# A hand-ordered attention and max-out kernel: its list of units is replaced by another list

## The chip, the cores and the metric

The kernel runs on one core of a Trainium2 chip. The metric is the device time of one execution, in microseconds (us). Names of engines: PE is the matrix engine (PEld its weight loads), ACT the scalar engine, DVE the vector engine, POOL the general one, and SP the engine that here does nothing but give out transfers (DMAs).

## What is computed

Local attention with a few global keys, in 4 batches of 8 heads, 768 positions and 64 columns a head, and after it a layer that takes the maximum of three products and multiplies it by a fourth matrix:

```python
scores = scale * np.matmul(q, k.transpose(0, 1, 3, 2))
is_global = pos[None, :] < 8
is_local = (rel >= 0) & (rel < 96)
dist = np.where(is_global & ~is_local, 96.0, np.abs(rel))
scores = np.where(is_global | is_local, scores - slopes * dist, -1e9)
a = softmax(scores)                     # over the keys
x = np.matmul(a, v)                     # then [4 * 768, 8 * 64] = [3072, 512]
h = np.maximum(np.maximum(x @ w1, x @ w2), x @ w3)   # 512 -> 768
out = h @ w_out                         # 768 -> 512
```

## The kernel before

**Tiles.** The 3072 rows are 24 tiles of 128; tile T is batch T // 6, position T % 6 in it. A query tile needs only its own key tile and the one before it (96 local keys), and the 8 global keys, which are copied over the first 8 places of the previous key tile. For the second layer the tiles are gathered in 7 chunks, of 4, 2, 2, 4, 4, 4 and 4 tiles.

**Units.** The whole work is cut in small units. A string, `SCHEDULE` (L25), lists them by name, and the loop at L475 calls them one by one: this is the order of instructions on each engine, written out by hand, and each engine works through its own part of it in that order. So a unit that waits holds up all that stands behind it on the same engine, and on SP a transfer that waits holds up the later ones. Numbers behind a letter are the unit's arguments; the last one often names the engine of a copy (0 ACT, 1 DVE, 2 POOL).

| unit | line | what it does |
|---|---|---|
| l, L, v, w, o | 151, 160, 169, 412, 419 | SP: loads of q or k in parts (tiles 0 to 11), of q and k of one tile (tiles 12 to 23; two transfers), of v, of w1, w2, w3 (w0.j: 512 KB, w1.j: 1 MB), of w_out |
| c, C, W, Q | 178, 185, 425, 429 | casts to bf16 of these: c of a part, C T.0 of a tile's q and k (3: half on DVE, half on POOL), C T.1 of its v, W of w, Q of w_out |
| x | 226 | PE: 8 transposes of a part of q or k, then one copy to SBUF (0 and 2: ACT, 1 and 3: DVE) or two half copies, ACT and DVE (4 and up) |
| X | 245 | the same for a tile: 4 is a transpose by DMA, given out by SP; below 4 it is 8 transposes on PE and copies (1: DVE; 3: one half each on ACT and DVE) |
| S | 268 | PE: scores of four heads (g) of a tile; ACT: exp. With a last digit 1 the bias is added on PE first, with 0 the mask is left to M |
| M | 302 | DVE: exp of the scores times the mask |
| G, V | 209, 218 | copies of the 8 global keys or values into a tile's buffers, between the tile's own use and the next tile's |
| A | 311 | PE: attention times v; DVE: reciprocal and multiply (L331, L332), which give xb |
| T | 335 | transposes xb into the chunk's xT: 4 by DMA from SP, else 4 transposes on PE and a copy |
| F c.f.j | 355 | PE: product of chunk c with columns f of w1, w2 or w3 (j); j = 0: ACT copies it to h01; j = 1 and 2: DVE takes the maximum |
| O c.t | 385 | PE: a tile's product with w_out, six matmuls; copy by ACT or DVE; SP: store |
| E | 390 | the same for the last chunk, cut finer |
| B, K | 291, 297 | the bias and mask tables |
| D i.n | 432 | n matmuls of zeros, 128 columns each, whose result nobody reads |

**Buffers that tie units together.** F, O, D and some transposes share three PSUM buffers (psH, L116); one more is for transposes (psT, L117). Scores and A share two (sp0, sp1; the last digit of A says which). Six raw buffers take q and k (L103), six take v, five take the casts, three xb, six P (two a tile), four the stores.

Of the kernel before, what the change touches and what calls it, by code (L numbers as in the profile page):

```python
# [22 lines left out]


SCHEDULE = """  # L25
    B6.1 K5 B5.1 D0.54 l1.0 K6 c1.0.2 B4.1 B0.1 B2.1 K0 B3.0 B7.1 B1.1 c0.1.1 c0.0.0 x0.0.3 K4 x0.1.4 K7
    S0.1.1 S0.0.1 l1.1 c1.1.1 G0.0 S1.1.0 v0 C0.1.1 S1.0.1 G1.1 x1.0.3 M0.1 M0.0 x1.1.4 A0.1 M1.0 v1 v2
    S2.0.1 S2.1.0 G2.2 M1.1 S3.0.1 S3.1.1 C1.1.1 C2.1.2 M2.0 M2.1 l2.1 c2.1.1 A1.0 V1.2 K1 x2.1.4 v3
    T0.1 C3.1.2 A2.1 V2.0 l2.0 c2.0.0 G3.0 w0.0 T1.0 A3.0 x2.0.4 M3.0 w0.1 T2.0 T3.1 w0.2 W0.0.2 W0.2.1
    W0.1.2 S4.0.0 S4.1.0 M4.1 G4.0 F0.0.0 F0.1.0 F0.1.1 K2 F0.0.1 S5.0.0 S5.1.0 V3.2 w1.0 W1.0.1 F0.0.2  # L30
    K3 M5.0 F0.1.2 F0.3.0 M4.0 F0.2.0 w1.1 W1.1.1 W2.0.2 F0.5.0 F0.4.0 W2.1.2 F0.5.1 v4 C4.1.2 A4.0
    F0.4.1 M5.1 F0.3.1 w1.2 W2.2.0 W1.2.2 T4.1 V4.2 F0.2.1 M3.1 F0.5.2 v5 C5.1.0 A5.0 l3.1 c3.1.2 F0.3.2
    F0.2.2 T5.1 l3.0 c3.0.0 x3.1.3 F0.4.2 F1.0.0 F1.4.0 x3.0.4 F1.0.1 F1.0.2 l3.2 c3.2.2 x3.2.3 l3.3
    c3.3.2 F1.3.0 x3.3.1 G6.1 F1.2.0 F1.1.0 F1.1.1 S7.1.0 S7.0.0 G7.2 F1.2.1 F1.4.1 F1.1.2 F1.3.1 S6.1.0
    S6.0.0 F1.2.2 F1.5.0 o0 Q0.2 M6.1 o2 o1 v7 C7.1.2 M7.0 v6 C6.1.0 S8.1.0 S8.0.0 Q2.2 M6.0 v11 l4.1 v8
    v9 Q1.2 G8.1 l4.0 F1.3.2 M7.1 F1.5.1 F1.5.2 O0.2.0 M8.1 A6.1 T6.4 v10 A7.0 V7.2 T7.4 F1.4.2 L12 M8.0
    O0.0.0 S9.1.0 S9.0.0 c4.1.2 x4.1.4 O0.3.0 M9.1 c4.0.2 M9.0 L13 O0.1.0 L14 x4.0.4 C8.1.2 A8.1 F2.0.0
    F2.1.0 C11.1.0 F2.3.0 C10.1.1 T8.4 G9.2 S10.0.0 S10.1.0 C9.1.2 F2.1.1 V8.1 F2.0.1 F2.1.2 A9.0 V9.2
    G10.0 M10.0 F2.3.1 F2.3.2 S11.1.0 M11.1 M10.1 S11.0.0 M11.0 C12.0.2 O1.1.0 F2.2.0 F2.0.2 A10.0
    F2.2.1 V10.0 T9.4 F2.5.0 A11.1 F2.4.0 C13.0.2 X13.4 F2.2.2 T10.1 v13 X12.4 F2.5.1 G12.2 C14.0.2  # L40
    O1.0.0 T11.1 F2.4.1 F2.4.2 F3.0.0 F3.1.0 F3.0.1 F3.0.2 F3.1.1 F3.1.2 C13.1.1 v17 L15 C15.0.3
    S13.1.0 M13.1 v18 S13.0.0 M13.0 F3.3.0 G13.0 F3.2.0 F3.2.1 S12.0.0 S12.1.0 F3.2.2 F3.3.1 v12 C12.1.0
    A13.1 V13.2 v14 X14.4 L16 F2.5.2 F3.3.2 M12.1 C14.1.2 S14.0.0 M14.0 M12.0 S14.1.0 M14.1 F3.4.0
    F3.4.1 F3.5.0 L18 v15 A12.1 A14.0 X15.4 F3.4.2 L17 C17.1.2 C15.1.0 T12.4 C18.0.2 v16 C16.1.2 G14.1
    C18.1.2 T13.4 F3.5.1 T14.4 F3.5.2 C16.0.0 S15.1.0 M15.1 S15.0.0 X16.4 X18.4 G15.1 V14.1 L19 O3.2.1
    O3.1.0 M15.0 O3.3.0 C17.0.2 A15.1 V15.1 X17.4 O2.0.0 T15.1 S16.0.0 C19.0.2 S16.1.0 M16.1 O3.0.1
    M16.0 F4.0.0 F4.2.0 S18.1.0 L20 S18.0.0 C20.0.2 F4.0.1 F4.0.2 F4.4.0 A16.0 X19.4 L21 F4.5.0 M18.0
    F4.5.1 F4.5.2 G16.0 T16.4 S17.1.0 S17.0.0 F4.2.1 v19 v20 V16.0 X20.4 M18.1 C19.1.2 M17.1 M17.0
    F4.2.2 F4.1.0 F4.1.1 S19.1.0 S19.0.0 M19.1 L22 F4.3.0 C21.0.0 X21.4 M19.0 O2.1.1 F4.3.1 A18.1 T18.4
    A17.0 C22.0.0 T17.4 G18.1 F4.1.2 G19.2 F4.3.2 A19.1 T19.4 V19.2 v21 L23 F4.4.1 F4.4.2 S20.0.0 M20.0  # L50
    S20.1.0 G20.0 X22.4 O4.2.0 C23.0.2 X23.4 M20.1 C20.1.0 O4.0.0 S21.1.0 S21.0.0 M21.1 F5.0.0 F5.1.0
    A20.1 F5.2.0 F5.3.0 F5.2.1 G21.0 S22.1.0 M21.0 S22.0.0 G22.2 V20.2 M22.1 F5.1.1 F5.0.1 C21.1.1
    F5.0.2 M22.0 S23.1.0 S23.0.0 F5.4.0 F5.3.1 F5.4.1 F5.4.2 F5.2.2 T20.4 v23 v22 A21.0 C22.1.2 F5.1.2
    V21.2 M23.0 A22.1 T22.4 V22.1 M23.1 F5.3.2 C23.1.0 O4.1.0 F5.5.0 A23.1 T23.4 F5.5.1 T21.4 F5.5.2
    O5.0.0 O4.3.0 O5.2.0 F6.0.0 F6.4.0 F6.4.1 O5.3.1 F6.2.0 F6.2.1 O5.1.1 F6.2.2 F6.4.2 F6.0.1 F6.0.2
    F6.3.0 F6.3.1 F6.3.2 F6.5.0 F6.1.0 F6.1.1 F6.1.2 F6.5.1 F6.5.2 E D1.9
"""


# [450 lines left out]
```

## Time and profile before

| | |
|---|---|
| median of 3 runs | 188.74 us (188.74 to 188.77) |
| the profiled execution | 188.74 us, its span 187.0 us |
| DMA packets, bytes | 88931, 36.83 MB, mean 197 GB/s |
| SP's queue, share of 16 engines' time | 86.8% |
| F units on PE, 128x512 form | 347 matmuls recorded, 379 ns each |
| transposes by DMA | 12 of q and k (2.07 us of SP each, 4.5 us to land), 15 of xb (1.26 us, 2.8 us) |
| transposes on PE | 96 of q and k parts, 36 of xb |

The span runs from the first to the last instruction. "Busy" for PE is the time in which a matmul is in flight; matmuls overlap, so in a row the 379 ns of one take only some 0.216 us of PE's time (38 in 8.37 us). An arrow "A <- B: 4.9, 4, 1.9" says that A waited for B for 4.9 us in all, 4 times, 1.9 us at the longest. Columns of a stage line are told where it is shown.

### The profile page before, as it was taken

How to read it: one execution, taken by the hardware profiler on the slowest of the kernel's cores; microseconds unless marked ns; L12 is line 12 of the kernel's file. 1: busy time of each engine (PE TensorE's matmuls, PEld its weight loads, DVE VectorE, ACT ScalarE, POOL GpSimd, SP SyncE). 2: the span in 40 equal slices, each digit the busy share in tenths (PEclk: the TensorE clock that was granted, in tenths of full speed). 3: DMA queues.
4: the chain of work that ended last, by engine and by line, in shares of the span. 5: the costliest groups of instructions: out<-in, count | busy, mean ns of one | idle time of the engine just before them, and what ended most of it. 6: DMA issues, size and time to landing. Idle time of an engine off the chain costs nothing.

```text
span 187.0 us, 4000 instructions
## 1 busy us (share of the span) xinstructions
PE 169.2 (91%) x1550; PEld 99.1 (53%) x1571; DVE 126.0 (67%) x241; ACT 96.9 (52%) x155; POOL 37.9 (20%) x62
## 2 busy tenths in 40 slices
PE   7787899999999899999989699999859999999991
PEld 7653754558765678545545345454424554444450
DVE  5767868898799789478985257897457793256500
ACT  5677887623675675337645454644937322311240
POOL 4102426442527040021130420211021200000000
PEclk9997899999999999999999999999999999999999
DMA  5999999999885999999999999999797415220023
GB/s 142 290 236 233 303 383 342 320 360 308 211 199 137 186 294 174 230 222 167 226 208 140 181 287 261 148 220 242 157 167 171 85 44 152 112 112 4 0 100 126
DMA packets 88931, 36.83 MB, mean 197 GB/s; under 512 B 71504, under 2 KB 83664, under 8 KB 88912
## 3 DMA queue, kind: packets, MB, share of 16 engines
q1 hardware_dynamic: 88768, 36.51, 86.8%
q8 instruction: 12, 0.20, 0.4%
q14 instruction: 7, 0.06, 0.1%
q10 hardware_dynamic: 144, 0.07, 0.1%
HBM read 25.17 MB, written 6.29 MB: 168 GB/s over the span
## 4 chain that ended last, share of the span: by engine, by line
PE 46%; DMA 19%; DVE 18%; issue 7%; SPq 4%; ACT 3%; POOL 1%; ACTq 0%; DVEq 0%; POOLq 0%
PE h L361 30%; PE po L376 7%; DMA qkT<-qkb 6%; DVE qkT L243 4%; DMA xT<-xb 4%; PE sp L283 4%; DVE P L307 3%; DMA out_dram<-ost 3%; DVE xb L332 3%; DMA rawp<-in_k_dram 3%; SPq L167 3%; DVE ht L370 3%; DMA raw<-in_k_dram 3%; DVE h L368 2%; ACT P L288 2%
## 5 line engine op out<-in xcount | busy, mean ns | idle before, releaser
L361 PE MATMUL h<-xT,w 128*128 128x512 bf16 (+1 forms) x491 | 100.2, 348 | 2.4 <-DMA xT<-xb 1.4
L361 PEld LDWEIGHTS <-w 128*128 128x128 bf16 x504 | 46.8, 98 | 42.0 <-issue 2.3
L288 ACT ACTIVATE P<-sp 128x1024 bf16<-128x1024 f32 (+1 forms) x48 | 43.4, 953 | 19.2 <-PE sp L283 19.1
L368 DVE TENSOR_TENSOR h<-h,h 128x512 bf16<-128x512 bf16 (+1 forms) x42 | 25.4, 606 | 21.2 <-PE h L361 20.8
L307 DVE TENSOR_TENSOR P<-P,wmask 128x1024 bf16<-128x1024 bf16 x36 | 28.5, 799 | 11.8 <-ACT P L288 11.2
L366 ACT CAST h<-h 128x512 bf16<-128x512 f32 (+1 forms) x42 | 22.0, 530 | 26.6 <-PE h L361 25.9
L376 PE MATMUL po<-wo,ht 128*128 128x512 bf16 (+2 forms) x148 | 32.9, 362 | 0.8 <-DVE ht L370 0.2
L370 DVE TENSOR_TENSOR ht<-h,h 128x512 bf16<-128x512 bf16 (+1 forms) x42 | 25.3, 606 | 3.4 <-PE h L361 1.8
L382 ACT COPY ost<-po 128x512 f32<-128x512 f32 (+2 forms) x20 | 11.2, 563 | 24.2 <-PE po L376 22.5
L376 PEld LDWEIGHTS <-ht 128*128 128x128 bf16 x156 | 14.2, 98 | 15.5 <-DVE ht L370 1.0
L283 PE MATMUL sp<-qkT 64*128 64x128 bf16 x352 | 15.0, 219 | 7.7 <-DMA qkT<-qkb 4.9
L283 PEld LDWEIGHTS <-qkT 64*128 64x128 bf16 x352 | 10.3, 95 | 17.5 <-DMA qkT<-qkb 6.9
L332 DVE TENSOR_TENSOR xb<-op,rz 128x512 bf16<-128x512 f32 x24 | 16.6, 691 | 0.8
L322 PEld LDWEIGHTS <-P 128*128 128x128 bf16 x192 | 12.7, 99 | 3.0 <-issue 0.5
L322 PE MATMUL op<-va,P 128*128 128x65 bf16 x160 | 13.1, 196 | 0.3 <-DVE P L307 0.3
L198 POOL CAST qkb<-raw 128x1024 bf16<-128x1024 f32 x8 | 8.3, 1038 | 23.3 <-DMA raw<-in_k_dram 23.3
L189 POOL CAST va<-rawv 128x512 bf16<-128x512 f32 x11 | 7.3, 664 | 23.8 <-DMA rawv<-in_v_dram 19.4
L325 PEld LDWEIGHTS <-P 128*128 128x128 bf16 x160 | 10.9, 99 | 1.2
L243 DVE COPY qkT<-tpp 128x512 bf16<-128x512 bf16 (+1 forms) x12 | 10.6, 906 | 0.7 <-PE tpp L239 0.5
L325 PE MATMUL op<-va,P 128*128 128x65 bf16 x128 | 10.0, 193 | 0.3 <-ACT va L221 0.3
L382 DVE COPY ost<-po 128x512 f32<-128x512 f32 (+1 forms) x6 | 3.7, 621 | 7.3 <-PE po L376 5.7
L239 PE MATMUL tpp<-identb,qkp 128*128 128x128 bf16 x96 | 7.6, 227 | 0.6 <-ACT qkp L183 0.3
(64 smaller groups left out, 107.8 us busy)
## 6 DMA issues: line engine op xcount, KB each, us to landing
rawv<-in_v_dram SPq DMA_DIRECT2D x24, 256.0 KB, 5.6
out_dram<-ost SPq DMA_DIRECT2D x23, 256.0 KB, 3.0
rawp<-in_q_dram SPq DMA_DIRECT2D x6, 512.0 KB, 7.2
rawp<-in_k_dram SPq DMA_DIRECT2D x6, 512.0 KB, 7.1
wst<-in_moe_w_dram SPq DMA_DIRECT2D x3, 1024.0 KB, 12.1
raw<-in_q_dram SPq DMA_DIRECT2D x12, 256.0 KB, 4.5
raw<-in_k_dram SPq DMA_DIRECT2D x12, 256.0 KB, 5.0
wst<-in_moe_w_dram SPq DMA_DIRECT2D x3, 512.0 KB, 6.6
```

The costliest lines, as they stand in the source:

```text
L243: copy(dst[:, lo:hi], tp.rearrange("c e j i -> c j i e"))
L283: nc.tensor.matmul(sp[:, hh, j2, ds], qT(T - ds, 1)[hsl, jp], qT(T, 0)[hsl, jp], start=not how, stop=True, skip_group_check=True)
L288: nc.scalar.activation(P[:, :, 0:n], sp.rearrange("p a b d n -> p (a b) d n")[:, :, 0:n], AF.Exp, bias=0.0, scale=scale)
L307: nc.vector.tensor_mul(P, P, wmask[:, g, :, 0:2])
L322: nc.tensor.matmul(o, P[:, i, 0], heads(va[T])[:, h], start=True, stop=(t == 0), skip_group_check=True)
L325: nc.tensor.matmul(o, P[:, i, 1], heads(va[T - 1])[:, h], start=False, stop=True, skip_group_check=True)
L332: nc.vector.tensor_tensor(out=x.rearrange("p (g h) d -> p g h d", g=2), in0=o4[:, :, :, 0:64], in1=rz[:, :, :, None].to_broadcast([128, 2, ...
L361: nc.tensor.matmul(ps, w123[f // 2][:, dm, j, (f % 2) * 128:(f % 2) * 128 + 128], xT[c][:, dm], start=(dm == 0), stop=(dm == 3))
L366: nc.scalar.copy(h01, ps)
L368: nc.vector.tensor_max(h01s[c, f], h01s[c, f], ps)
L370: nc.vector.tensor_max(ht[c][:, f], h01s[c, f], ps)
L376: nc.tensor.matmul(po, ht[c][:, f, tt * 128:(tt + 1) * 128], wo[:, f, cols], start=(f == 0), stop=(f == NF - 1))
```

## The change

The string is replaced by another; no other line differs. The same units stand in it, but for the zero matmuls: D0.54 at the head and D1.9 at the end become D0.45 at the head and D1.4 between x0.0 and x0.1. The order is another throughout, and so are many engine digits:

| | before | after |
|---|---|---|
| X by DMA / on PE | 12 / 0 | 9 / 3 (X12.1, X16.3, X18.3) |
| T by DMA / on PE | 15 / 9 | 11 / 13 |
| x: ACT whole / DVE whole / halves | 0 / 5 / 7 | 6 / 3 / 3 |
| c by ACT / DVE / POOL | 3 / 3 / 6 | 1 / 4 / 7 |
| C of q and k, ACT / DVE / POOL / half and half | 3 / 0 / 8 / 1 | 2 / 3 / 7 / 0 |
| C of v, ACT / DVE / POOL | 7 / 5 / 12 | 10 / 4 / 10 |
| W, ACT / DVE / POOL | 1 / 3 / 5 | 4 / 2 / 3 |
| V that copy, ACT / DVE / POOL | 3 / 4 / 9 | 0 / 2 / 14 |
| A in sp0 / sp1 | 11 / 13 | 10 / 14 |

On SP the first loads stand as l1.0 l1.1 v0 v1 v2 l2.1 v3 l2.0 w0.0 w0.1 w0.2 w1.0 w1.1 before, and as l1.0 l1.1 v0 l2.0 l2.1 v1 v2 v3 w0.0 w1.0 w0.1 w0.2 v4 w1.1 after (l0.0 and l0.1 stand ahead of the list, in both). The diff, with parts of the old list left out and the new one whole:

```diff
-    B6.1 K5 B5.1 D0.54 l1.0 K6 c1.0.2 B4.1 B0.1 B2.1 K0 B3.0 B7.1 B1.1 c0.1.1 c0.0.0 x0.0.3 K4 x0.1.4 K7
-    S0.1.1 S0.0.1 l1.1 c1.1.1 G0.0 S1.1.0 v0 C0.1.1 S1.0.1 G1.1 x1.0.3 M0.1 M0.0 x1.1.4 A0.1 M1.0 v1 v2
-    S2.0.1 S2.1.0 G2.2 M1.1 S3.0.1 S3.1.1 C1.1.1 C2.1.2 M2.0 M2.1 l2.1 c2.1.1 A1.0 V1.2 K1 x2.1.4 v3
-    T0.1 C3.1.2 A2.1 V2.0 l2.0 c2.0.0 G3.0 w0.0 T1.0 A3.0 x2.0.4 M3.0 w0.1 T2.0 T3.1 w0.2 W0.0.2 W0.2.1
-    W0.1.2 S4.0.0 S4.1.0 M4.1 G4.0 F0.0.0 F0.1.0 F0.1.1 K2 F0.0.1 S5.0.0 S5.1.0 V3.2 w1.0 W1.0.1 F0.0.2
-    K3 M5.0 F0.1.2 F0.3.0 M4.0 F0.2.0 w1.1 W1.1.1 W2.0.2 F0.5.0 F0.4.0 W2.1.2 F0.5.1 v4 C4.1.2 A4.0
-    F0.4.1 M5.1 F0.3.1 w1.2 W2.2.0 W1.2.2 T4.1 V4.2 F0.2.1 M3.1 F0.5.2 v5 C5.1.0 A5.0 l3.1 c3.1.2 F0.3.2
-    F0.2.2 T5.1 l3.0 c3.0.0 x3.1.3 F0.4.2 F1.0.0 F1.4.0 x3.0.4 F1.0.1 F1.0.2 l3.2 c3.2.2 x3.2.3 l3.3
-    c3.3.2 F1.3.0 x3.3.1 G6.1 F1.2.0 F1.1.0 F1.1.1 S7.1.0 S7.0.0 G7.2 F1.2.1 F1.4.1 F1.1.2 F1.3.1 S6.1.0
...
-    A13.1 V13.2 v14 X14.4 L16 F2.5.2 F3.3.2 M12.1 C14.1.2 S14.0.0 M14.0 M12.0 S14.1.0 M14.1 F3.4.0
-    F3.4.1 F3.5.0 L18 v15 A12.1 A14.0 X15.4 F3.4.2 L17 C17.1.2 C15.1.0 T12.4 C18.0.2 v16 C16.1.2 G14.1
-    C18.1.2 T13.4 F3.5.1 T14.4 F3.5.2 C16.0.0 S15.1.0 M15.1 S15.0.0 X16.4 X18.4 G15.1 V14.1 L19 O3.2.1
...
-    C18.1.2 T13.4 F3.5.1 T14.4 F3.5.2 C16.0.0 S15.1.0 M15.1 S15.0.0 X16.4 X18.4 G15.1 V14.1 L19 O3.2.1
-    O3.1.0 M15.0 O3.3.0 C17.0.2 A15.1 V15.1 X17.4 O2.0.0 T15.1 S16.0.0 C19.0.2 S16.1.0 M16.1 O3.0.1
-    M16.0 F4.0.0 F4.2.0 S18.1.0 L20 S18.0.0 C20.0.2 F4.0.1 F4.0.2 F4.4.0 A16.0 X19.4 L21 F4.5.0 M18.0
-    F4.5.1 F4.5.2 G16.0 T16.4 S17.1.0 S17.0.0 F4.2.1 v19 v20 V16.0 X20.4 M18.1 C19.1.2 M17.1 M17.0
-    F4.2.2 F4.1.0 F4.1.1 S19.1.0 S19.0.0 M19.1 L22 F4.3.0 C21.0.0 X21.4 M19.0 O2.1.1 F4.3.1 A18.1 T18.4
-    A17.0 C22.0.0 T17.4 G18.1 F4.1.2 G19.2 F4.3.2 A19.1 T19.4 V19.2 v21 L23 F4.4.1 F4.4.2 S20.0.0 M20.0
-    S20.1.0 G20.0 X22.4 O4.2.0 C23.0.2 X23.4 M20.1 C20.1.0 O4.0.0 S21.1.0 S21.0.0 M21.1 F5.0.0 F5.1.0
-    A20.1 F5.2.0 F5.3.0 F5.2.1 G21.0 S22.1.0 M21.0 S22.0.0 G22.2 V20.2 M22.1 F5.1.1 F5.0.1 C21.1.1
-    F5.0.2 M22.0 S23.1.0 S23.0.0 F5.4.0 F5.3.1 F5.4.1 F5.4.2 F5.2.2 T20.4 v23 v22 A21.0 C22.1.2 F5.1.2
-    V21.2 M23.0 A22.1 T22.4 V22.1 M23.1 F5.3.2 C23.1.0 O4.1.0 F5.5.0 A23.1 T23.4 F5.5.1 T21.4 F5.5.2
-    O5.0.0 O4.3.0 O5.2.0 F6.0.0 F6.4.0 F6.4.1 O5.3.1 F6.2.0 F6.2.1 O5.1.1 F6.2.2 F6.4.2 F6.0.1 F6.0.2
-    F6.3.0 F6.3.1 F6.3.2 F6.5.0 F6.1.0 F6.1.1 F6.1.2 F6.5.1 F6.5.2 E D1.9
+    K0 K1 K2 K3 K4 K5 l1.0 l1.1 D0.45 c0.0.2 B0.1 B1.1 B2.1 B3.0 K6 B4.1 B5.1 c0.1.1 c1.0.2 x0.0.4 B6.1
+    B7.1 D1.4 x0.1.4 S0.0.1 v0 l2.0 l2.1 K7 S0.1.1 G0.0 S1.0.1 S1.1.0 x1.0.3 c1.1.2 M0.0 M0.1 M1.0 v1
+    x1.1.4 C0.1.2 v2 A0.1 G1.2 S2.0.1 M1.1 c2.0.2 x2.0.1 C1.1.1 S2.1.0 G2.2 S3.0.1 M2.0 M2.1 C2.1.1 T0.1
+    S3.1.1 M3.0 M3.1 c2.1.2 v3 A1.0 C3.1.0 w0.0 V1.2 x2.1.2 w1.0 A2.1 V2.2 A3.0 T1.0 T2.1 T3.1 W1.0.1
+    W0.0.0 G3.2 S4.0.0 S4.1.0 F0.0.0 F0.1.0 M4.0 F0.2.0 F0.3.0 G4.1 S5.0.0 M4.1 S5.1.0 w0.1 W0.1.1 w0.2
+    W0.2.2 V3.2 F0.0.1 F0.1.1 F0.0.2 F0.1.2 v4 C4.1.0 A4.0 V4.2 w1.1 W1.1.2 W2.0.0 F0.4.0 F0.5.0 M5.0
+    M5.1 w1.2 W1.2.2 v5 W2.1.0 T4.0 F0.2.1 F0.3.1 l3.0 l3.2 F0.4.1 l3.1 c3.0.2 c3.2.2 F0.5.1 o2 C5.1.0
+    A5.1 l3.3 F0.2.2 Q2.2 F0.3.2 W2.2.0 o0 T5.0 F0.4.2 o1 F0.5.2 x3.0.0 F1.0.0 F1.1.0 c3.1.1 F1.2.0
+    x3.2.0 Q0.2 F1.0.1 F1.1.1 F1.2.1 l4.0 l4.1 c3.3.0 F1.0.2 F1.1.2 F1.2.2 x3.1.2 x3.3.1 F1.3.0 F1.4.0
+    Q1.2 F1.3.1 S6.0.0 S6.1.0 v6 v7 v8 G6.0 F1.3.2 F1.5.0 v9 c4.0.1 F1.4.1 S7.0.0 S7.1.0 G7.2 v10 M6.0
+    M6.1 M7.0 M7.1 O0.0.0 F1.4.2 c4.1.1 C6.1.2 C7.1.2 L12 F1.5.1 S8.0.0 S8.1.0 x4.0.0 O0.1.0 A6.0 x4.1.2
+    A7.1 V7.2 F1.5.2 v11 T6.0 O0.2.0 T7.1 G8.2 C8.1.2 S9.0.0 S9.1.0 G9.1 v12 v13 O0.3.0 F2.0.0 F2.1.0
+    S10.0.0 M8.0 M8.1 M9.0 M9.1 S10.1.0 C9.1.2 L13 L14 F2.0.1 F2.1.1 F2.0.2 A8.0 C12.0.1 F2.1.2 G10.2
+    O1.0.0 V8.2 A9.1 X12.1 M10.0 M10.1 C10.1.0 C11.1.0 F2.2.0 S11.0.0 S11.1.0 M11.0 M11.1 L15 F2.3.0
+    F2.4.0 O1.1.0 V9.2 A10.1 F2.2.1 V10.2 T8.0 F2.3.1 F2.5.0 T9.0 A11.1 F2.4.1 T10.0 F2.2.2 F2.3.2 T11.1
+    F2.4.2 S12.0.0 S12.1.0 F2.5.1 C13.0.2 C14.0.2 C15.0.1 X13.4 F3.0.0 F3.1.0 F3.0.1 G12.1 C12.1.0
+    F3.2.0 F3.1.1 F3.2.1 S13.0.0 S13.1.0 F2.5.2 v14 C13.1.0 C14.1.2 M12.0 M12.1 F3.0.2 F3.1.2 X14.4
+    F3.2.2 X15.4 G13.2 M13.0 M13.1 S14.0.0 S14.1.0 F3.3.0 F3.4.0 F3.5.0 M14.0 M14.1 G14.1 A12.0 A13.1
+    F3.3.1 F3.4.1 F3.5.1 S15.0.0 M15.0 S15.1.0 G15.0 v15 V13.2 L16 L17 v16 T12.4 v17 M15.1 O2.0.0
+    C15.1.0 A14.0 V14.2 F3.3.2 F3.4.2 T13.4 F3.5.2 C16.1.0 C16.0.2 X16.3 T14.4 C17.0.2 A15.1 X17.4
+    O2.1.0 S16.0.0 S16.1.0 G16.1 L18 V15.2 L19 T15.1 M16.0 O3.0.0 M16.1 F4.0.0 F4.1.0 F4.0.1 F4.1.1
+    C18.0.2 L20 C19.0.2 A16.1 F4.2.0 F4.3.0 S17.0.0 S17.1.0 F4.2.1 F4.0.2 F4.3.1 v18 M17.0 v19 M17.1
+    X18.3 X19.4 C20.0.0 V16.2 F4.1.2 C17.1.2 O3.1.1 A17.1 F4.2.2 F4.3.2 S18.0.0 M18.0 S18.1.0 M18.1
+    F4.4.0 T16.4 T17.4 F4.4.1 C18.1.2 C19.1.1 F4.4.2 X20.4 G18.1 S19.0.0 S19.1.0 F4.5.0 L21 M19.0 M19.1
+    v20 F4.5.1 A18.0 T18.4 F4.5.2 A19.1 T19.4 V19.1 C21.0.1 X21.4 G19.1 L22 C22.0.2 L23 X22.4 O3.2.1
+    O3.3.0 O4.0.1 S20.0.0 S20.1.0 M20.0 G20.0 O4.1.0 F5.0.0 F5.1.0 F5.2.0 S21.0.0 S21.1.0 G21.2 F5.0.1
+    F5.1.1 M20.1 M21.0 F5.3.0 F5.0.2 F5.1.2 F5.2.1 F5.2.2 v21 C20.1.1 C21.1.2 F5.4.0 S22.0.0 M21.1
+    S22.1.0 C23.0.0 F5.3.1 M22.0 M22.1 F5.5.0 F5.3.2 A20.0 V20.2 G22.2 v22 F5.4.1 X23.4 v23 F5.5.1 T20.4
+    A21.1 V21.1 T21.4 F5.4.2 F5.5.2 S23.0.0 S23.1.0 M23.0 O4.2.0 M23.1 C22.1.2 A22.0 C23.1.0 O4.3.0
+    V22.2 T22.4 A23.1 T23.4 O5.0.1 O5.1.0 O5.2.1 O5.3.0 F6.0.0 F6.1.0 F6.0.1 F6.0.2 F6.2.0 F6.3.0 F6.4.0
+    F6.1.1 F6.2.1 F6.1.2 F6.3.1 F6.4.1 F6.2.2 F6.3.2 F6.5.0 F6.4.2 F6.5.1 F6.5.2 E
```

More of the change, by code (lines that the diff above doesn't have):

```diff
@@ L31 @@
-    K3 M5.0 F0.1.2 F0.3.0 M4.0 F0.2.0 w1.1 W1.1.1 W2.0.2 F0.5.0 F0.4.0 W2.1.2 F0.5.1 v4 C4.1.2 A4.0
-    F0.4.1 M5.1 F0.3.1 w1.2 W2.2.0 W1.2.2 T4.1 V4.2 F0.2.1 M3.1 F0.5.2 v5 C5.1.0 A5.0 l3.1 c3.1.2 F0.3.2
-    F0.2.2 T5.1 l3.0 c3.0.0 x3.1.3 F0.4.2 F1.0.0 F1.4.0 x3.0.4 F1.0.1 F1.0.2 l3.2 c3.2.2 x3.2.3 l3.3
-    c3.3.2 F1.3.0 x3.3.1 G6.1 F1.2.0 F1.1.0 F1.1.1 S7.1.0 S7.0.0 G7.2 F1.2.1 F1.4.1 F1.1.2 F1.3.1 S6.1.0
-    S6.0.0 F1.2.2 F1.5.0 o0 Q0.2 M6.1 o2 o1 v7 C7.1.2 M7.0 v6 C6.1.0 S8.1.0 S8.0.0 Q2.2 M6.0 v11 l4.1 v8
@@ L36 @@
[L36 to L40, printed above, removed]
@@ L41 @@
-    O1.0.0 T11.1 F2.4.1 F2.4.2 F3.0.0 F3.1.0 F3.0.1 F3.0.2 F3.1.1 F3.1.2 C13.1.1 v17 L15 C15.0.3
-    S13.1.0 M13.1 v18 S13.0.0 M13.0 F3.3.0 G13.0 F3.2.0 F3.2.1 S12.0.0 S12.1.0 F3.2.2 F3.3.1 v12 C12.1.0
-    A13.1 V13.2 v14 X14.4 L16 F2.5.2 F3.3.2 M12.1 C14.1.2 S14.0.0 M14.0 M12.0 S14.1.0 M14.1 F3.4.0
-    F3.4.1 F3.5.0 L18 v15 A12.1 A14.0 X15.4 F3.4.2 L17 C17.1.2 C15.1.0 T12.4 C18.0.2 v16 C16.1.2 G14.1
-    C18.1.2 T13.4 F3.5.1 T14.4 F3.5.2 C16.0.0 S15.1.0 M15.1 S15.0.0 X16.4 X18.4 G15.1 V14.1 L19 O3.2.1
```

## The prediction

> **What bounds the kernel now.** I read the page's busy times and slices first, then busy time by stage, then TensorE's waits, the chain that ended last, and last the rows that price single operations. The profiled execution took 188.74 us, which is also the median of the three runs; its span is 187.0 us, so 1.74 us lie around the span. I add my sum to 188.74.
>
> ```profile
> PE 169.2 (91%) x1550; PEld 99.1 (53%) x1571; DVE 126.0 (67%) x241; ACT 96.9 (52%) x155; POOL 37.9 (20%) x62
> PEclk9997899999999999999999999999999999999999
> DMA  5999999999885999999999999999797415220023
> ```
>
> PE is busy for most of the span and no other engine is near it; but the DMA row stands at its top until slice 30 of 40. Two resources are tight, PE and the transfers. The stages (columns: stretch and length; then busy us and count for PE, PEld, DVE, ACT, POOL; clock; DMA):
>
> ```profile
> 0.00:24.10 24.10, 19.39 (x258) 15.22 (x259) 16.52 (x44) 17.46 (x29) 6.59 (x19) 0.93 1.01 245
> 24.10:63.40 39.30, 37.49 (x363) 23.32 (x368) 34.06 (x59) 23.69 (x38) 16.37 (x21) 1.00 0.96 270
> 63.40:107.40 44.00, 40.43 (x400) 24.55 (x407) 30.57 (x63) 23.21 (x38) 9.08 (x13) 1.00 1.17 208
> 107.40:158.80 51.40, 47.92 (x404) 24.26 (x410) 34.95 (x61) 26.13 (x40) 5.89 (x10) 1.00 0.86 176
> 158.80:182.40 23.60, 23.49 (x124) 11.44 (x124) 9.63 (x14) 6.13 (x11) 0.00 (x0) 1.00 0.18 66
> ```
>
> I cut them at F0.0.0 (24.1), F2.0.0 (63.4), F4.0.0 (107.4) and F6.0.0 (158.8). PE idles 1.8, 3.6 and 3.5 us in the middle three, 8.9 together, and not at all in the last. So work added to PE after 24.1 is paid in full, and at most 8.9 us can be won there. What the idle time waits for:
>
> ```profile
> PE sp L283 <- DMA qkT<-qkb: 4.9, 4, 1.9
> PE h L361 <- DMA xT<-xb: 1.4, 2, 0.8
> PE sp L283 <- DVE qkT L243: 1.4, 3, 0.9
> ```
>
> 4.9 + 1.4 = 6.3 us are waits for transposes that the DMA makes; 8.9 - 6.3 = 2.6 us are the rest, mostly DVE. In the chain the late part runs through transfers (start, us, what):
>
> ```profile
> 113.39 6.53 DMA qkT<-qkb
> 119.97 0.62 PE sp L283 x16
> ...
> 134.35 5.39 DMA qkT<-qkb
> 139.79 0.62 PE sp L283 x16
> ```
>
> **Transposes moved to PE: +2.6 us.** X has 9 DMA transposes instead of 12, T 11 instead of 15. Each X on PE is 8 transposes, which the chain prices at 0.57 us ("PE tpp L239 x8"); each T is 4, at 0.22 ("PE xtp L349 x4"). 3 x 0.57 + 4 x 0.22 = 2.6, all on PE behind 24.1, where nothing hides it. The copies they need (0.59 us on ACT, 0.42 to 1.2 on DVE) go to engines with gaps.
>
> **Engines exchanged: 0 by themselves.** Counting the schedule words by their engine digit and taking the mean of each row, ACT gets about 8 us more (x of 0 and 2 are whole copies, four W casts, seven T copies), DVE about 2 less, POOL about 1.6 less. ACT then stands near 105 of 187. Its cover is its own gaps (25.9 us waiting for h, 22.5 for po); without it some of the 8 us would show as late h01 copies.
>
> **The transfers: -2.8 us.** SP gives out 7 transposes fewer: its rows give 2.07 us for an X and 1.26 for a T, so 3 x 2.07 + 4 x 1.26 = 11.2 us of SP's time fall away. SP was issuing almost without a gap from 77 to 136, so this is real relief. Against it stands one serial stretch that the new order makes: T17.4, X20.4, L21, v20, T18.4, T19.4, X21.4, L22, L23, X22.4 stand in this order on SP, each behind a wait. From the start of A17: 0.5 for A, 0.9 for its reciprocal and multiply, 1.3 to issue T17.4, 2.1 for X20.4, so L21 starts near 4.8. T19.4 waits for A19, which PE reaches 8.7 us after A17 by the row means; its xb is there at 10.1 and SP is free for X21.4 at 11.4. X21.4 takes 2.1; then L22, whose second half starts at 14.1 and lands 5.0 later (the row's median), 1.04 for the cast on POOL, and X22.4 from 20.2, landing 4.5 later: 24.7. PE has 25.1 us of work between A17 and S22. By medians it just fits, and with the same sum for S23 (exp 2.05, cast 1.05, X 4.5 against 7.0 us of PE work) and for v21 the waits come to 0.6 us. But landings scatter:
>
> ```profile
> DMA to landing us min/median/max: 3.1/4.5/6.5
> ```
>
> for X, and up to 5.5 for T. The bounds are 0.6 us (all medians) and 6.3 (as much as before). I take the middle, 3.5: the relief is real, but X21 to X23 hang on each other with 0.4 us to spare. 3.5 - 6.3 = -2.8; bounds -5.7 and 0.
>
> **First weights and the head: +0.4 us.** SP's first fifteen loads are the same set, reordered: l2.0 and l2.1 go ahead of v1 to v3, w1.0 ahead of w0.1 and w0.2. w1.0 (1 MB) now lands when w0.1 and w0.2 together did, no later than the DVE cast at 25.16 that waited for it. W1.0.1 stands on DVE ahead of M4.0, G4.1, M4.1 and W0.1.1: 25.2 + 0.8 + 0.8 + 0.25 + 0.8 + 0.7 = 28.5, while PE, from 24.1 with four F units of 0.863 and S5 of 0.62, wants W0.1 at 28.2. F0.2.0 waits 0.1, F0.0.1 0.3. The start of F0.0.0 I leave at 24.1: v3 issued last, at 13.8, plus 5.6 to land and 0.6 to cast gives 20.0, before A3's 20.9; W0.0.0 was cast from 22.2 on and needs 1.05. Bounds: -0.9 (F0 right behind W0.0.0) and +1.5 (v1 to v3 land as late as the slowest v, 12.0 us). The zero matmuls: 45 + 4 for 54 at the head, at 0.107 each, end before the first transposes can start (load landed 5.42, cast 1.04). The nine at the end of before stand behind the last output matmul, at 182.4; taking them off changes nothing.
>
> The clock is part of these bounds. It fell to half from 17.0 to 20.0:
>
> ```profile
> 8.00:16.00 8.00, 5.62 (x81) 3.19 (x78) 6.08 (x11) 6.12 (x10) 1.48 (x3) 1.00 1.27 252
> 17.00:20.00 3.00, 3.00 (x37) 2.34 (x36) 1.87 (x5) 2.40 (x4) 0.92 (x2) 0.50 0.99 243
> ```
>
> PE had been busy 70% of the eight us ahead, with no wait over 1.2 us. PE's gaps ahead of 16 us come from the same casts and copies in the new order, so I leave the dip as it is: 0, with 1.5 us to win if it goes (3.0 us at half speed).
>
> [...]
>
> **Order of the F units: +1.7 us.** The new order puts units of one j together (F0.2.1 F0.3.1 F0.4.1 F0.5.1 F0.2.2 ...), and DVE's own list gets longer blocks of masks, xb and copies between two maxima. While DVE is in such a block, three h banks fill at 0.86 us each; what exceeds 2.6 us can stop PE. Summing each block by its rows (mask 0.80, xb 0.89, copies 0.42 to 1.22), the parts over 2.6 us come to 7.8 us before and 12.8 after, with the longest at A9 to A10 (6.2 us, ahead of F2.2.1) and M13 to A13 (5.2, ahead of F3.3.1). Before lost 2.6 us to such waits; 2.6 x 12.8 / 7.8 = 4.3, so +1.7. Bounds 0 (O units and attention cover them: PE has 6.0 us of other work beside the longest) and +5.0 (the whole difference).
>
> **Sum.** 2.6 - 2.8 + 0.4 + 1.7 = +1.9; 188.74 + 1.9 = 190.6. With single terms at their bounds it runs from about 188.9 to 193.5, the forecast's own range.
>
> **Rivals.** (a) Faster: SP's relief decides. With transfer waits at their medians (0.6) and all DVE blocks covered (0 more), 188.74 + 2.6 - 5.7 + 0.4 = 186.0. For it speak the 11.2 us off SP and the chain through transfers from 85 to 140; against it the 0.4 us of slack at X22. It decides once PE's waits behind 24.1 fall under 8.9 - 2.6 - 0.4 = 5.9 us. (b) The serial stretch L21, X21, L22, X22, X23 becomes the bound: if X21 to X23 land like the chain's 6.53 and 5.39 rather than 4.5, some 1.5 us each, 4.5 more: 195.1. Before had just such landings there; against it, less is queued. (c) The order does nothing in sum, gain and loss cancel: 188.7.
>
> **Chances.** Runs lie within 0.03 us, so 0.2% (0.4 us) can be told. Forecast 0.48, (b) 0.24, (a) 0.20, (c) 0.08. Slower 0.48 + 0.24 = 0.72; same 0.08; faster 0.20. The range takes in most of (a) and (b): 186.3 to 195.2.
>
> **What would show it.** PE's transposes up by 40 matmuls; S behind DMA waiting under 4.9 us in all, and what is left lying at S21 to S23; F0.0.1 waiting on the W0.1 cast; F2 and F3 waiting on DVE, DVE full there. It is wrong in sign if F6.0.0 starts ahead of 161.4 (158.8 and the 2.6 us of O5.3 and O5.1, which now stand before it); its terms are wrong if F0.0.0 starts far from 24.1, or if SP's queue is late for another reason than X.

## The result, and the profile after

The new list takes 180.78 us (median; 180.64 to 180.97) where the old one takes 188.75 on the same chip: 0.9578 of it, interval 0.956 to 0.9597. It is faster by 4.2%; slower was forecast. The profiled execution of it took 180.64 us, with a span of 178.9. The old list scatters from run to run and from chip to chip (medians of 187.8 to 190.2), the new one hardly; so the experiments below are told by their ratio to the old list on their own chip.

The page of the new kernel (busy time by engine; two rows of slices):

```profile
PE 168.6 (94%) x1575; PEld 98.8 (55%) x1597; DVE 118.7 (66%) x237; ACT 103.1 (58%) x160; POOL 37.7 (21%) x65
...
PEclk9999999999999999999999999999999999999999
DMA  4999999999999699999544899586899864700015
```

PE's share rises to 94%, the clock stays at full speed, and the DMA row is no longer at its top all through. The stages, cut at the same units as before (F0.0.0, F2.0.0, F4.0.0, F6.0.0, the end of the last matmul), with the same columns:

```profile
0.00:23.48 23.48, 18.13 (x254) 13.39 (x254) 14.97 (x41) 17.11 (x28) 9.43 (x23) 1.00 0.99 247
23.48:60.59 37.11, 36.84 (x357) 23.32 (x361) 27.29 (x52) 28.00 (x42) 12.82 (x17) 1.00 1.07 304
60.59:100.51 39.92, 39.55 (x429) 25.01 (x434) 30.91 (x65) 25.64 (x43) 7.80 (x13) 1.00 0.83 174
100.51:154.32 53.81, 53.28 (x436) 26.97 (x442) 36.96 (x69) 25.92 (x38) 7.66 (x12) 1.00 0.85 180
154.32:174.90 20.58, 20.48 (x104) 9.91 (x105) 8.24 (x12) 6.01 (x11) 0.00 (x0) 1.00 0.16 58
```

From F0.0.0 to F6.0.0 PE idles 0.3 + 0.4 + 0.5 = 1.2 us where it idled 8.9. All waits of PE that the profile lists (those over 0.15 us; engine and line, what it waited for, us, times, longest):

```profile
PE wp L436 <- DVE tiny L443: 1.2, 1, 1.2
PE op L322 <- DVE va L189: 0.8, 1, 0.8
PE tpp L239 <- POOL qkp L183: 0.8, 1, 0.8
PE tpp L239 <- ACT qkT L243: 0.7, 1, 0.7
PE xtp L349 <- DVE xb L332: 0.6, 1, 0.6
PE op L322 <- ACT P L288: 0.4, 1, 0.4
PE op L322 <- DVE rz L331: 0.4, 1, 0.4
PE sp L283 <- ACT qkT L243: 0.2, 1, 0.2
PE h L361 <- issue: 0.2, 1, 0.2
```

No wait for a DMA is left, and what is left lies ahead of F0.0.0, but for the last line. ("issue" is time in which PE waited for nothing that the profile shows.) The chain that ended last says the same by its shares:

```profile
PE 83%; SPq 6%; DMA 6%; DVE 1%; issue 1%; ACT 1%; POOL 0%; ACTq 0%
```

It was 46% PE and 19% DMA.

**Where the 8.1 us of span went.** F0.0.0 starts at 23.5 for 24.1: -0.6. From F0.0.0 to F6.0.0 it takes 130.8 for 134.8, so -3.9. PE's idle time falls by 7.7 in it, from 8.9 to 1.2, and its busy time grows by 3.8, though two O units more (2.6) and the added transposes (2.4 by their rows) stand in it; the 1.2 us between 3.8 and 5.0 are not explained. From F6.0.0 to the end it takes 24.6 for 28.1; less the two O units that is -1.0. These 1.0 us lie behind the last output matmul (4.6 us to the end of the span before, 3.6 after); why is not shown.

The -0.6 is the clock's, not the order's. In the old profile the clock is at half from 17 to 20 us. In five other profiles with the same units up to F0.0.0 and the clock full there (e2, e8, e10, e15, e18) F0.0.0 starts at 22.7 to 23.1, that is 1.0 to 1.4 us sooner (in a sixth, e13, at 24.2, behind a wait of 1.3 us for a cast of w0); in the profiles whose head is the new list's it starts at 23.2 to 23.6. At full clock the new head is the later one, by some 0.5 us.

Why do the DMA transposes not wait any more? SP's own timeline, old kernel, from X13 to X15 (start, us to give out, line, what):

```profile
72.87 1.98 SPq L250 DMA_TRANSPOSE qkT<-qkb  x1
74.91 0.57 SPq L174 DMA_DIRECT2D rawv<-in_v_dram  x1
75.53 1.46 SPq L250 DMA_TRANSPOSE qkT<-qkb  x1
77.12 0.50 SPq L383 DMA_DIRECT2D out_dram<-ost  x1
77.66 0.44 SPq L174 DMA_DIRECT2D rawv<-in_v_dram  x1
78.14 0.70 SPq L167 DMA_DIRECT2D raw<-in_q_dram  x1
78.89 1.61 SPq L167 DMA_DIRECT2D raw<-in_k_dram  x1
80.94 3.43 SPq L174 DMA_DIRECT2D rawv<-in_v_dram  x3
84.48 2.15 SPq L250 DMA_TRANSPOSE qkT<-qkb  x1
86.67 1.40 SPq L167 DMA_DIRECT2D raw<-in_q_dram  x1
88.12 0.58 SPq L167 DMA_DIRECT2D raw<-in_k_dram  x1
88.74 0.98 SPq L167 DMA_DIRECT2D raw<-in_q_dram  x1
89.77 1.26 SPq L167 DMA_DIRECT2D raw<-in_k_dram  x1
91.07 1.21 SPq L174 DMA_DIRECT2D rawv<-in_v_dram  x1
92.39 2.27 SPq L250 DMA_TRANSPOSE qkT<-qkb  x1
```

and the same three in the new kernel:

```profile
72.50 1.41 SPq L250 DMA_TRANSPOSE qkT<-qkb  x1
73.97 0.57 SPq L174 DMA_DIRECT2D rawv<-in_v_dram  x1
74.63 3.55 SPq L250 DMA_TRANSPOSE qkT<-qkb  x2
```

Both start X13 near 72.7. The old queue then has loads of tiles 16, 17 and 18 between, and comes to X15 at 92.4, when S15 wants it at 96.4; the new one has X14 and X15 out by 78.2. And they land sooner: the summary of all DMA transposes of q and k in the new kernel,

```profile
DMA to landing us min/median/max: 3.1/3.2/5.1
```

where the median was 4.5. Taken one by one, in the old profile an X with loads given out in the 4 us ahead of it landed after 3.7 to 6.5 us (eight of them), one without after 3.1 to 3.9 (four); a T with loads in the 3 us ahead of it after 4.0 to 5.5 (six), the others after 2.4 to 2.8, but for one of 4.2.

Late landing is one part; when they are given out is the other. In the old list the X for which S15, S16 and S22 waited went out 4.8, 3.3 and 5.4 us ahead of the start of their S; X16's landing, 3.3 us, was a quick one, it only went out too late. In the new list X13 to X20 go out 8.4 us ahead or more, and X21 to X23, 4.2 to 4.4 us ahead, land 0.5 to 1.1 us before their S starts.

### The profile page after: what moved, and what is told of

The parts are those of the page before. It is cut to its first block, busy times and chain, and to the rows that moved or that the text cites. A ratio compares the mean times of both kernels' runs of the same rounds, so it can differ in the third digit from the quotient of the medians.

```text
span 178.9 us, 4055 instructions
## 1 busy us (share of the span) xinstructions
PE 168.6 (94%) x1575; PEld 98.8 (55%) x1597; DVE 118.7 (66%) x237; ACT 103.1 (58%) x160; POOL 37.7 (21%) x65
## 4 chain that ended last, share of the span: by engine, by line
PE 83%; SPq 6%; DMA 6%; DVE 1%; issue 1%; ACT 1%; POOL 0%; ACTq 0%
PE h L361 53%; PE po L376 16%; PE sp L283 6%; DMA rawv<-in_v_dram 4%; SPq L158 4%; PE op L322 3%; PE op L325 2%; SPq L174 2%; PE tpp L239 2%; PE xtp L349 1%; DMA out_dram<-ost 1%; DVE xb L332 1%; ACT ost L382 1%; PE tp L261 1%; DVE rz L331 0%
## 5 line engine op out<-in xcount | busy, mean ns | idle before, releaser
L307 DVE TENSOR_TENSOR P<-P,wmask 128x1024 bf16<-128x1024 bf16 x36 | 24.6, 711 | 3.9 <-ACT P L288 3.8
L322 PEld LDWEIGHTS <-P 128*128 128x128 bf16 x192 | 12.4, 97 | 4.6 <-DVE va L189 1.2
L322 PE MATMUL op<-va,P 128*128 128x65 bf16 x160 | 12.5, 193 | 1.3 <-DVE va L189 0.8
L221 POOL COPY va<-vaf 8x260 int32<-8x260 int32 x14 | 6.5, 462 | 34.4 <-PE op L325 34.4
L198 POOL CAST qkb<-raw 128x1024 bf16<-128x1024 f32 x7 | 7.1, 1035 | 27.9 <-DMA raw<-in_k_dram 27.9
L325 PEld LDWEIGHTS <-P 128*128 128x128 bf16 x160 | 10.5, 97 | 1.4
L325 PE MATMUL op<-va,P 128*128 128x65 bf16 x128 | 9.9, 193 | 0.0
L243 ACT COPY qkT<-tpp 128x1024 bf16<-128x1024 bf16 (+1 forms) x9 | 7.9, 873 | 3.2 <-PE tpp L239 3.2
L183 POOL CAST qkp<-rawp 128x1024 bf16<-128x1024 f32 x7 | 7.3, 1040 | 8.5 <-DMA rawp<-in_q_dram 7.2
```

Source lines behind the costliest of these rows:

```text
L307: nc.vector.tensor_mul(P, P, wmask[:, g, :, 0:2])
L322: nc.tensor.matmul(o, P[:, i, 0], heads(va[T])[:, h], start=True, stop=(t == 0), skip_group_check=True)
L325: nc.tensor.matmul(o, P[:, i, 1], heads(va[T - 1])[:, h], start=False, stop=True, skip_group_check=True)
```

## The experiments

**Which transposes, by what.** Two theories at first: relief (SP gives out seven fewer) and order. The edits:

```diff
 e1, in the new list:
-X12.1 X16.3 X18.3 T6.0 T7.1 T8.0 T9.0
+X12.4 X16.4 X18.4 T6.4 T7.4 T8.4 T9.4
 e2, in the old list, the reverse
```

> The new list with the seven moved transposes given back to the DMA: X12, X16, X18 and T6 to T9 with digit 4, all else as in the new list. PE loses 40 transposes (2.6 us of work by the row means). Theory 'relief' (PE's 6.3 us of waits for DMA transposes went because SP gives out seven fewer): the waits come back, 184 us or more, and S or F wait for the DMA for 4 us or more. Theory 'order' (the waits went because of where the units stand, whatever makes the transposes): 178.5 to 182 us, since PE saves up to 2.6 and loses little by waiting. Theory 'zeros and clock': about 181, for it says nothing of these.

> The old list with the same seven transposes put on PE (X12.1, X16.3, X18.3, T6 to T9 by the new digits), all else as in the old list. 'Relief': 188.7 + 2.6 - 6.3 = 185 or less, with PE's waits for qkT and xT under 2 us. 'Order': 187 to 191, the added 2.6 us of PE work paid and at most as much won back. 'Zeros and clock': 191 (188.7 + 2.6).

e1: 186.2 us, 0.982 (0.975 to 0.989): 5.0 us more than e3 below, which is the new list but for its zero matmuls, on the same chip. That is as much as relief said. But its waits for the DMA lie on the seven themselves (F2.0.0 2.0, F3.0.0 2.4, S16 1.8):

```profile
PE h L361 <- DMA xT<-xb: 4.4, 2, 2.4
PE sp L283 <- DMA qkT<-qkb: 1.7, 1, 1.7
```

Nothing waits for the twenty others, and they land as fast as in the new list (X: 3.3 us). e2: 191.6 us, 1.010 (1.004 to 1.016), worse by about what PE's work grew. Its waits for the DMA are gone, as relief said, but others stand in their place:

```profile
PE xtp L349 <- DVE xb L332: 2.2, 2, 1.2
PE tp L261 <- ACT qkT L263: 1.7, 1, 1.7
```

and with seven fewer in the queue the X that are left land after 4.4 us, no sooner than the old 4.5:

```profile
DMA to landing us min/median/max: 3.1/4.4/6.0
```

Nor are they given out sooner: X15 goes out at 94.9 us (92.4 in the old list), X22 at 137.9 (134.4). S meets them in time only because PE itself comes later (F4.0.0 starts at 113.2 for 107.5). So relief by number has fallen. In the new list the seven stand right ahead of their use; to have them on PE is worth some 5 us there, and nothing in the old order.

**The zero matmuls.** e3 is the new list with D0.54, no D1.4, and D1.9 at the end; e4 the old list with D0.45, D1.4 behind x0.0 and no D1.9.

> The new list with the old zero matmuls: 54 at the head, none between the first two transposes, 9 at the end. 'Zeros and clock': the clock falls to half again for some 3 us before 24 and the time is 1.0 to 1.5 us longer, 182 or more. 'Order': within 0.4 us of 180.8 and the clock at 1.0, for the dip came from the old order's gaps between 8 and 16 us.

> The old list with the new zero matmuls: 45 at the head, 4 between x0.0 and x0.1, none at the end. 'Zeros and clock': the dip of 17 to 20 us goes and the time falls by 1.0 to 1.5 us to about 187.5. 'Order': within 0.4 us of 188.7, the dip stays.

e3: 181.2, 0.957 (0.951 to 0.964), as 'order' said: the zeros are worth nothing that can be told in the new list, and the clock is full there with the old ones. e4: 187.2, 0.990 (0.983 to 0.997), with no dip. That looks like the zeros' gain by the clock, but e2 and e8, which keep the old 54, show full clock between 17 and 20 us too. The dip in the old profile comes in some executions and not in others; the zeros don't decide it. Nor is it all of e4's gain: e4's three executions at full clock took 186.9 to 187.2 us, the old list's four on that chip 187.8 to 189.3. What the rest comes from is open.

**Order or digits.** e5 is the new order with every engine digit of the old list, e6 the old order with those of the new.

> The new list's order with every engine digit of the old list (casts, copies, transposes, the score buffer of A). 'Order' alone: 181 to 183 us. 'Digits' (which engine does what, the seven transposes among it): 186 to 189, as before. If both are needed, between, or worse than both, since digits chosen for one order block queues in another.

> The old list's order with every engine digit of the new list. 'Order': 188 or more. 'Digits': 181 to 184. If both are needed: 186 or more.

217.3 (1.157; 1.146 to 1.167) and 224.2 (1.194; 1.181 to 1.206): far worse than either. Order and digits can't be priced apart. My reading is that a digit decides which queue a unit blocks, and that this is good or bad by its neighbours: PE's longest waits are now for casts and copies (in e5 7.3 us for a weight cast on DVE and 4.1 for an output copy on ACT, in e6 5.6 for a copy of qkT on ACT) and for an exp on ACT (e6, 4.5). Not every single digit was tried.

**Stage by stage.** A prefix of one list, then what is left of the other in its own order: cut at F2.0.0 (e7 new head, e8 old head) and at F4.0.0 (e14 new, e15 old).

> The new list up to its F2.0.0 (60.6 us in the new profile), then what is left of the old list in the old order with the old digits. The traces give the new list 2.9 us at this point; if that is kept and the rest is independent, 185.9 us. If the old rest is bound by SP's queue and not by what PE has done, the lead is lost in waits for transposes: 188 or more. If the head sets up what comes later (loads further on), 183 or less.

> The old list up to its F2.0.0 (63.5 us), then what is left of the new list in the new order with the new digits. If stages are independent: 180.8 + 2.9 = 183.7 us. If the new rest needs the loads that the new head has given out, 185 or more.

> The new list up to its F4.0.0 (100.5 us), then what is left of the old list. Theory 'spread' (each stretch of the old order loses its own few us): the old rest loses what the old profile shows behind F4.0.0, 0.6 + 0.4 + 1.8 of waits for transposes, less 0.7 of work moved: 182.5 to 184.5 us. Theory 'lead' (the old rest loses only because SP's queue comes to it late; with a head that has given out its loads in time it runs clean): within 0.7 us of the new list.

> The old list up to its F4.0.0 (107.5 us), then what is left of the new list. 'Spread': the old part keeps its loss (waits of 0.8 at F2, 0.8 at S15, 1.9 at S16, others, and the clock's dip where it falls), the rest is clean: 184 to 186.5 us. 'Lead': the new rest inherits a late queue and waits too: 186.5 or more.

| | up to F2 | F2 to F4 | from F4 | us | ratio to the old list (interval) |
|---|---|---|---|---|---|
| new | new | new | new | 180.8 | 0.958 (0.956 to 0.960) |
| e8 | old | new | new | 183.1 | 0.975 (0.965 to 0.984) |
| e7 | new | old | old | 183.3 | 0.978 (0.968 to 0.989) |
| e14 | new | new | old | 186.5 | 0.982 (0.977 to 0.987) |
| e15 | old | old | new | 189.7 | 0.998 (0.994 to 1.001) |

Cut at F2.0.0 the gains of the two parts, 2.5% and 2.2%, add up to the whole 4.2% within their intervals, so nothing here speaks against independent parts (e8 came close to the 183.7 us expected for these; e7 was 2.6 us better than its 185.9). Cut at F4.0.0 they are 1.8% and 0.2%. But e14 has a seam of its own: S18 follows right on an X18 by DMA and waits 2.9 us (1.5%). Without that it would take some 183.6 us, within the range of 'spread'; so this cut can't tell. e15 against e8 is the clearest pair: the old order from F2 to F4, behind the old head, costs 2.3%, some 4.4 us. In it the waits of the old profile are back (F2 1.3, then S14, S15 and S16, 3.1 in three), and the new rest behind it wins nothing. e15 meets the number of 'lead', but not its reason: the new rest waits for DVE (S20 1.1, A17 0.8), not for a late queue. The old stretch from F2 to F4 takes 42.5 us behind the new head (e7), 44.0 in the old list and 47.4 in e15: it is cheaper behind the new head, and neither 'spread' nor 'lead' holds as written.

**Grouping of the F units.** e9 is the new list with the F of chunks 1 to 6 in the old list's order.

> The new list with its F units of chunks 1 to 6 in the old list's order: the k-th F of a chunk in the new list is replaced by the k-th F of that chunk in the old one, so the units of one j no longer stand together; all else stays. 'Grouping costs' (my term of +1.7 for longer blocks of DVE work): 179 to 180.4 us. 'Grouping gains' (two or three F of one j in a row keep DVE's queue free of waits): 182 or more, with PE waiting for DVE. Neither: within 0.4 of 180.8.

183.5, 0.978 (0.974 to 0.982): 2.7 us above the new list's 180.8 (e12 below, the new list but for one load, took 180.5 on the same chip). The grouping gains. The largest single wait that e9 brings is an output matmul (O1.1) behind a maximum, in place of none,

```profile
PE po L376 <- DVE h L368: 0.7, 1, 0.7
```

and x3.1 and S15 wait 0.4 and 0.3 more. Another 0.4, at F0.2.0 and F0.0.1, is for casts of weights; chunk 0 has the same order in both lists, and an execution of the unchanged list (e17) has 0.9 of it. So the grouping is worth 2.3 to 2.7 us, and the listed waits make up only part of that.

**The order on SP alone.** Three repairs of the old list, one spoiling of the new:

```diff
 e10, old list: X14 X15 T12 T13 X19 T16 X20 X22, each put ahead of the loads just before it; L22 behind X21
 e13, old list: only X14 X15 X19 X20 X22
 e18, old list:
-v17 L15 ... v18 v12 v14 X14.4 L16 ... L18 v15 X15.4 L17 C17.1.2 T12.4 C18.0.2 v16 C18.1.2 ... X16.4 X18.4 L19 ... X17.4
+L15 ... v12 v14 X14.4 L16 ... v15 X15.4 T12.4 v16 ... X16.4 L17 v17 C17.1.2 L18 v18 L19 ... X17.4 C18.0.2 X18.4 C18.1.2
 e11, new list: v14 v15 L16 v17 L18 L19 L21 v20 L22, each put ahead of the transposes it stood behind
```

> The old list with eight DMA transposes moved ahead of the loads that stood just before them on SP (X14, X15, T12, T13, X19, T16, X20, X22), and L22 put behind X21. PE's order, the digits and the number of transposes stay. Theory 'queue' (a DMA transpose given out right behind loads lands 1 to 3 us later, and PE's waits come from that): the median landing of X falls from 4.5 to 3.6 us or less, PE's waits for qkT and xT from 6.3 to 2.5 us or less, the time to 184 to 186.5 us. Theory 'number' (there are too many transposes): landings and waits as before, 188 to 189. Rival to both (loads given out later then land too late, or SP waits for an xb ahead of a load): waits move to the casts, 188 or more.

> The old list with only X14, X15, X19, X20 and X22 ahead of the loads that stood just before them; no T is moved, so SP does not come to wait for an xb ahead of a load, as it did when T12, T13 and T16 were moved too (there SP waited 9.7 us for one and the time was 190.4). 'Queue, place by place': S15's and S19's waits go, PE's waits for qkT fall under 3 us, 186 to 187.5 us. 'Late as a whole': the waits move to the next tile (S16, S22), 188 or more.

> The old list with its loads of tiles 17 and 18 (L17, v17, L18, v18, their casts and X18) put behind X16, so that SP comes to v12, v14, X14, X15 and X16 without them; nothing goes ahead of a load that PE needs sooner. 'Far loads ahead of near ones': X15 is given out some 4 us sooner than 92.4, X16 some 5 us sooner than 102, the waits of S15 (0.8) and S16 (1.9) go, and the time is 1.5 to 3 us under the old list of the same chip, if S18 does not wait for X18. 'Late as a whole': the waits appear at S17 and S18 instead, within 1 us of the old list.

> The mirror of it: the new list with loads put ahead of the DMA transposes they stood behind (v14, v15, L16, v17, L18, L19, L21, v20, L22). 'Queue': the median landing of X rises from 3.2 to 4 us or more, PE waits for DMA transposes for 1 to 3 us, 181.5 to 184 us. 'Number': as the new list, within 0.4 of 180.8.

e10: 190.4, 1.012 (1.004 to 1.019). X lands after 3.3 us now, as the queue theory said, and the waits of S15, S19, S22 and F5 are gone. Yet the time does not fall: S16 still waits 1.7 us, and new waits stand at A15 (0.9), S21 (1.2) and S23 (2.2), whose X23 had to wait for a load, L23, that landed at 138.9. (The wait of 9.7 us that the next expectation puts at T12 lies ahead of T22, near the end, where the old list has one of 8.5; ahead of T12 SP stood idle for 1.3 us.) e13, without any T: 192.4, 1.016 (1.011 to 1.022); its profile is of an execution of 194.7 us, the longest of six. S15's wait is gone, but v12 now comes late for A13, which reads it too, and S23 waits as in e10; its L23 was given out at 137.4, behind X22, where the old list gives it out at 132.4:

```profile
PE sp L283 <- DMA qkT<-qkb: 3.2, 1, 3.2
PE op L325 <- ACT vaf L189: 2.8, 1, 2.8
```

e18: 194.9, 1.034 (1.028 to 1.039). X15 goes out at 86.3 for 92.4 and X16 at 98.8, and S15 and S16 wait for nothing, as "far loads" said. But X18 then comes far too late, and more than was won is lost at S18:

```profile
PE sp L283 <- DMA qkT<-qkb: 10.6, 2, 10.3
```

e11: 181.4, 0.966 (0.962 to 0.971). The spoiled queue lands X after 4.5 us in the median, not 3.2:

```profile
DMA to landing us min/median/max: 3.1/4.5/6.0
```

and PE waits for one of them, 1.1 us at S21; the time is 0.6 us above the new list's 180.8, and 0.9 above e12 on the same chip. That settles one thing: loads ahead of a DMA transpose make it land later, and that alone costs little where it is given out well ahead of its S (5.4 to 9.2 us for X17, X19 and X20 in e11, 8.5 to 9.0 in the new list, 6.6 to 7.2 in the old).

**One improvement tried.** v1 ahead of l2.1 in the new list (e12; again as e16, beside the new list itself, e17).

> The new list with the load v1 ahead of l2.1 on SP. In the new profile A1 waits 0.84 us for the cast of v1 ahead of F0.0.0. If that wait sets the start of F0: 0.4 to 0.8 us less, 180.0 to 180.4. If the chain of exps or of w0.0 sets it: within 0.3 of 180.8.

> The new list with v1 ahead of l2.1, as run before, now beside the new list itself on one chip. If the 180.51 seen there is the edit: 0.2 to 0.4 us under the new list here. If it is the chip: no difference.

> The new list unchanged, as a yardstick on the same chip: 180.6 to 181.0 us.

e12: 180.5, 0.962 (0.957 to 0.966). Side by side e16 takes 180.75 (180.63 to 181.12) and e17 180.93 (180.71 to 181.68). Not told apart: A1's wait went, and x2.1 waited for its cast instead, 0.86 us. No version here beats the new list.

## Why the prediction was wrong

Against the forecast of 190.6 us the result is some 10 us lower: 3.5 by the transfers, 3.1 by the order of the F units, 1.0 by the head, 0.2 by the transposes on PE, and 2.2 that no term had.

- **The bound**: right. PE was the bound, and added work was paid in full. Of the 8.9 us of idle time behind 24.1, 7.7 went; I named that ceiling and then let no case reach it. No term had the 1.2 us by which PE's busy time grew less than the work added, nor the 1.0 us at the end.
- **Transposes on PE, +2.6**: right, 2.4 by rows and stages.
- **Engines exchanged, 0**: right as far as PE waited for none of them. ACT rose by 6.2 us; DVE fell by 7.3, not 2. Part of that is the masks (799 ns each before, 711 after); why they are quicker was not tried.
- **The transfers, -2.8**: the first step that failed. All 6.3 us of waits went, beyond the bound of -5.7. I worked the serial stretch L21, X21, L22, X22, X23 with the old medians (4.5 for an X) and took the middle between "fits" and "as before". But the old landings belonged to the old queue: with no load right ahead they are 3.1 to 3.9 for X20 to X23, and the stretch runs with 0.5 to 1.1 us to spare. The reason I gave, relief by seven fewer, fell with e2; what goes is the waiting on transposes given out too late, by their place (e18) and by their kind (e1) together.
- **First weights and head, +0.4**: its place in the sum came out as -0.6, inside the bounds given, but that is the clock: I took the dip as it was, and the new profile has none. At full clock the new head is later by some 0.5 us. The waits that I gave F0.2.0 and F0.0.1 (0.1 and 0.3) are absent in the new list's profile and there in e17's, an execution of the same list (0.3 and 0.6).
- **Order of the F units, +1.7**: the second step that failed, and in its sign. It scaled 2.6 us that I called mostly DVE's. The old profile's waits behind 24.1 that are not for a transpose by DMA, by the same view from there to 158.8, are these and 0.4 of "issue":

```profile
PE op L322 <- DVE P L307: 0.3, 1, 0.3
PE sp L283 <- DVE qkT L243: 0.3, 1, 0.3
PE h L361 <- DVE qkT L243: 0.3, 1, 0.3
PE po L376 <- DVE ht L370: 0.2, 1, 0.2
```

  That is 1.1 us, and 0.3 of it at an F unit; of the row of 1.4 that I showed for it, 1.1 lies ahead of 24.1. So there was little to scale. In the new profile none of the four is left: PE waits for DVE nowhere behind F0.0.0, though units of one j stand together. e9 puts that grouping at 2.3 to 2.7 us of gain.
- **The range**: with the transfers alone at their bound of -5.7 the sum is 187.7, not 188.9; even so the result lies far below. F6.0.0 started at 154.3, under the 161.4 that I had named as the sign of being wrong.
- **Rival (a)**, 186.0, had the sign and the term that decided. It fell short by 5.3: it kept 1.4 us of other idle time that went, 0.6 for transposes, +0.4 at the head where -0.6 came, 0.2 too much for the transposes on PE, and it had nothing for the 2.2 us that no term had.

What stays open: which few moves make the old order into a good one. Three repairs of its queue cured the waits they aimed at and raised others. That neither the order nor the digits alone bring the gain is shown (e5, e6, and e2 for the seven transposes); how much each transpose's earlier place is worth was not separated.

## What to carry to other kernels

Where a new order replaces another on a bound engine, the lowest time to allow for is work without any wait: all idle time of that engine may go at once, from several causes. A transfer's time to landing in the old trace is a property of its place in the queue; read it one by one, with what was given out just before, and do not carry the median into a new order. An order and its choice of engines are one solution: half of another, or a single repaired wait, can be worse than either.

## What the runs showed of the hardware that I had not expected

A DMA transpose of q and k landed 3.1 to 3.9 us after it was given out where no load stood right ahead of it, and up to 6.5 us behind loads (old profile); one of xb mostly 2.4 to 2.8, and behind loads up to 5.5 (5.7 in e10).

The clock fell to half, for 3.4 us at a time, without PE idling that long. In e2, e10, e13, e14 and e15 it did so 0.5 to 1.3 us after PE had waited 1.7 to 2.9 us, and once more in e13 during a wait of 3.2; in the old profile (0.50 from 17 to 20 us) after waits of 1.0 and 0.3 us, with PE busy 70% of the eight us ahead. (Waits of 4 to 10 us, in e5, e6 and e18, are left out here.) Other waits of 1.7 to 2.4 us passed without a dip (S16 and S22 in the old profile, F3.0.0 in e1), so no threshold can be read from these. So a short wait can cost more than itself: with the old profile's dip F0.0.0 came 1.0 to 1.4 us later than without. The Trainium skill, "TensorE: Matmul & The Clock Gate", Part 1, has the half clock come after an idle window of about 3.4 us; the dips told here came without one. The same Part also tells of a kernel whose clock went back and forth because PE idled briefly and often between groups of matmuls; whether that is what happens here is not shown. The new list's executions, beside the old list and as e17, had a mean clock of 0.996 to 1.0.
